# Bonus of a linear-attention chunk moved onto the diagonal of its score tile, with the ninth chunk prepared later and a new written order of the first stage

## The chip, the cores and the metric

The kernel runs on one core of one Trainium2 chip. The metric is the device time of one execution in microseconds. TensorE does the matrix products, VectorE (DVE) and ScalarE (ACT) the elementwise work, GpSimd (POOL) a small part of it, and SyncE (SP) issues most of the transfers. Each engine takes its instructions in the order in which they are written.

## The reference

Two steps follow each other. The first is a linear attention with a decay per channel and a bonus `u` for the current token; the second is a gated feed-forward layer on its output.

```python
for t in range(S):                      # S = 768, batch 4, 8 heads of 48
    cur = np.einsum('bhd,bhe->bhde', u[None] * kt, vt)
    y[:, :, t] = np.einsum('bhd,bhde->bhe', rt, state + cur)
    state = wt[:, :, :, None] * state + np.einsum('bhd,bhe->bhde', kt, vt)
gate = 1.0 / (1.0 + np.exp(-(x @ w_gate)))     # x: 3072 x 384, d_ff = 1536
return gate * (x @ w_val) @ w_out
```

All inputs are float32; the weights come as 64-bit floats and are decoded on the chip.

## The kernel before

Sequence and batch are cut into 24 chunks of 128 tokens; chunk q belongs to batch q % 4 and to row q // 4, so a row is the same 128 tokens of all four batches. Each chunk has two inputs: `pin` (decay, k and r with channels on partitions) and `tok` (r, k and v with tokens on partitions).

The work on one chunk goes in these steps. On DVE, `prep_k` scans the decays and scales k (lines 320 to 331), `fade` ages the state, `prep_r` scans again and scales r (339 to 347). On TensorE, `turn_k` turns k (354), and ACT copies it out (`take_k`). `scores` and `sums` make the score tile and the sums of k times v in the bank pair `pa` (367 to 393). `mask` on DVE multiplies the scores by a strict triangle into the tile `at` (443), `middle` and `keep` bring the state forward. `states` and `mix` (395 to 421) give the chunk's output `py`, `take_y` adds the bonus to it on DVE (463), `turn_x` turns it (467), `take_x` and `rest_x` leave it as a high and a low part in `x`. The bonus is the sum over each head of r, u and k, times v: `bonus1` and `bonus2` are products on POOL (305, 310), `bonus3` a sum on DVE (312), `bonus4` the product with v on POOL (316). `guard` on ACT squares the scans and keeps a sum that is checked at the end.

A row of the feed-forward layer goes over 12 slices f of the hidden dimension: `gate` and `value` (nine matmuls each into `pg` and `pu`), `sigmoid` on ACT, `hidden` on DVE, the split of the product into `hh` (ACT) and `hl` (DVE), and `down` (nine matmuls into `po`). `pg` and `pu` have one bank each.

**The first stage**, up to the end of row 0, is ordered by a planner (class `Plan`, lines 147 to 193). It starts, at each moment of its own reckoning, the ready operation with the lowest rank; ranks come from the list `TURNS` (chunks c and weight slices w), from `LAGS` for the two groups of the feed-forward layer in row 0, and `COMES` is the order of the transfers on SP. `ROOM` says how many buffers a tile has. In this stage each weight slice arrives as 64-bit words (`fetch`), is guarded on ACT (`w_guard`, two passes), decoded on DVE (`w_body`, `w_sign`, `w_tail`) and split (`w_hi` on ACT, `w_lo` on DVE). Chunks 0 to 7 are done here, and the preparation of chunk 8. Group 0 (batches 0 and 1) multiplies by whole float32 weights, line 502; group 1 (batches 2 and 3) by split ones, line 505.

**The loop** over rows 1 to 5 follows a fixed pattern (`blocks`, lines 670 to 706): a slice f has four slots (0 ahead of `gate`, 1 ahead of `value`, 2 ahead of `down` of the slice before, 3 behind it). Each chunk takes three slices; `both` (line 643) does the output of chunk q and the scores of chunk q + 1 among each other in slot 3 of the second slice, `turn_x` is in slot 2 of the third, and `prep_k` of the next chunk opens its first slice. Row 5 has no attention in it.

Of the kernel before, what the change touches and what calls it, by code (L numbers as in the profile page):

```python
# [197 lines left out]
def tile_kernel(ctx: ExitStack, tc: tile.TileContext, dec: bass.AP, tok: bass.AP, wts: bass.AP, u: bass.AP, out: bass.AP):  # L198
# [117 lines left out]
    def bonus4(q):  # L316
        a0 = bank["a0", q].unsqueeze(2).broadcast_to([P, H, D])
        nc.gpsimd.tensor_tensor(out=by_head(bon[q]), in0=by_head(tk[q][:, 2 * DM:]), in1=a0, op=ALU.mult)  # L318
# [124 lines left out]
    def mask(q):  # L443
        att[q] = p1.tile([P, 2, NP, HC], F32, tag="at", name=f"at{q}")
        found = bank["a", q][:, :, :NP * HC].rearrange("a o (p c) -> a o p c", c=HC)
        nc.vector.tensor_tensor(out=att[q], in0=found, in1=after.unsqueeze(1).unsqueeze(1).broadcast_to([P, 2, NP, HC]), op=ALU.mult)
# [16 lines left out]
    def take_y(q):  # L463
        mine = bon[q].rearrange("a (p o e) -> a o p e", o=2, e=D)
        nc.vector.tensor_tensor(out=mine, in0=bank["yy", q], in1=mine, op=ALU.add)  # L465
# [81 lines left out]
    def leave(n):  # L547
        o = stage.tile([P, NKT, B * C], F32, tag="o", name=f"o{n}")
        for j in range(NKT):
# [4 lines left out]
            nc.scalar.dma_start(out[n, j * P:(j + 1) * P], o[:, j])  # L554
# [217 lines left out]
```

## Time and profile before

| | us |
|---|---|
| median of 3 runs (range) | 589.24 (589.06 to 589.64) |
| the profiled execution, its own time | 589.89 |
| its span, first to last instruction | 588.1 |
| TensorE busy in the span | 552.6 (94%) |
| DVE busy | 332.9 (57%) |
| ACT busy | 193.8 (33%) |
| POOL busy | 94.5 (16%) |

The span lies 1.8 us inside the execution's own time. The first stage ends with the last `po` matmul of row 0 at 152.83 us of the span, where the first `pg` of row 1 starts; from there rows 1 to 4 take about 88 us each. Times in rows of the profile count from the span's start. "PEld" is the load of weights into TensorE, which lies beside the matmuls. In a row of the timeline the first number is the start, the second the duration, and the bracket at the end tells how long the engine was idle just before and what ended that.

### The profile page before, as it was taken

Reading aid. Unit: us, or ns where it says so; the run is one execution under the profiler, and the core shown is the slowest. Engines: PE = TensorE matmul, PEld = TensorE weight load, DVE = VectorE, ACT = ScalarE, POOL = GpSimd, SP = SyncE. Lnnn points to the kernel's source line nnn. Section 1 sums busy time; section 2 is a strip of 40 time slices with the busy share of each in tenths; the row PEclk is TensorE's granted clock in tenths of the full one; section 3 lists DMA queues with packets and bytes.
Section 4 is the critical chain, followed back from the end, with each engine's and each line's share of the span. In section 5 each row is a group of like instructions: output and inputs, shape, how many; then the busy total and the mean of one; then the engine's idle time right before and its main releaser. Section 6 shows DMA issues by size and latency. Waiting matters only on the chain.

```text
span 588.1 us, 13530 instructions
## 1 busy us (share of the span) xinstructions
PE 552.6 (94%) x6042; PEld 462.5 (79%) x6042; DVE 332.9 (57%) x485; ACT 193.8 (33%) x359; POOL 94.5 (16%) x86
## 2 busy tenths in 40 slices
PE   2399799999999999999999999999999999999995
PEld 2378588989888888788888788888788888788884
DVE  3989999998555645645645645645645632222121
ACT  2658783324322312322312322312322311311221
POOL 3324232111120210210210211211221200000000
PEclk9999999999999999999999999999999999999999
DMA  8999443305120221330230340230330200100001
GB/s 246 311 326 314 138 173 88 89 6 154 74 90 23 67 88 30 97 107 19 71 88 22 97 114 13 77 90 17 107 109 19 70 1 2 54 3 1 1 1 58
DMA packets 11188, 50.79 MB, mean 86 GB/s; under 512 B 1280, under 2 KB 1408, under 8 KB 9584
## 3 DMA queue, kind: packets, MB, share of 16 engines
q1 hardware_dynamic: 8528, 45.11, 25.0%
q10 hardware_dynamic: 2592, 4.72, 2.2%
q8 instruction: 49, 0.80, 0.6%
q14 instruction: 19, 0.16, 0.1%
HBM read 45.11 MB, written 4.72 MB: 85 GB/s over the span
## 4 chain that ended last, share of the span: by engine, by line
PE 81%; DVE 7%; DMA 4%; issue 3%; ACT 2%; POOL 1%; SPq 0%; ACTq 0%; DVEq 0%; POOLq 0%
PE pg L505 23%; PE pu L505 23%; PE po L545 21%; PE py L405 3%; PE py L418 3%; DMA tok<-tok 3%; PE pa L376 2%; DMA ub<-u 1%; PE pk L357 1%; DVE sg L523 1%; PE pa L389 1%; DVE temp L261 1%; DVE raw L264 1%; DVE w L275 1%; PE po L541 1%
## 5 line engine op out<-in xcount | busy, mean ns | idle before, releaser
L505 PE MATMUL pg<-x,w 128*128 128x512 f32 (+1 forms) x648 | 151.4, 377 | 0.2
L505 PE MATMUL pu<-x,w 128*128 128x512 f32 (+1 forms) x648 | 148.2, 373 | 1.1 <-DVE sg L523 1.1
L523 DVE TENSOR_TENSOR sg<-pu,sg 128x512 f32<-128x512 f32 (+1 forms) x84 | 51.6, 614 | 151.8 <-PE pu L505 143.1
L505 PEld LDWEIGHTS pu<-x,w 128*128 128x128 f32 x648 | 115.2, 188 | 22.6 <-DVE sg L523 1.3
L505 PEld LDWEIGHTS pg<-x,w 128*128 128x128 f32 x648 | 113.4, 188 | 23.4 <-DVE x L490 1.9
L545 PE MATMUL po<-hh,w 128*128 128x512 f32 (+1 forms) x432 | 128.9, 382 | 0.0
L516 ACT ACTIVATE sg<-pg 128x512 f32<-128x512 f32 (+1 forms) x84 | 45.0, 536 | 184.9 <-PE pg L505 175.4
L545 PEld LDWEIGHTS po<-hh,w 128*128 128x128 f32 x432 | 76.7, 189 | 12.7 <-ACT hh L527 0.2
L527 ACT CAST hh<-sg 128x512 fp32r<-128x512 f32 (+1 forms) x72 | 42.1, 584 | 135.1 <-DVE sg L523 135.1
L545 PE MATMUL po<-hl,w 128*128 128x512 f32 (+1 forms) x216 | 80.7, 374 | 0.0
L531 DVE TENSOR_TENSOR hl<-sg,hh 128x512 fp32r<-128x512 f32 (+1 forms) x72 | 49.1, 682 | 42.5 <-ACT hh L527 42.5
L307 POOL TENSOR_TENSOR bon<-tok,ub 128x384 f32<-128x384 f32 x24 | 29.6, 1235 | 228.4 <-DMA tok<-tok 186.5
L545 PEld LDWEIGHTS po<-hl,w 128*128 128x128 f32 x216 | 40.7, 188 | 8.0 <-DVE hl L531 0.4
L318 POOL TENSOR_TENSOR bon<-tok,a 128x384 f32<-128x384 f32 x24 | 23.1, 966 | 144.9 <-DVE a L314 144.9
L310 POOL TENSOR_TENSOR bon<-bon,tok 128x384 f32<-128x384 f32 x24 | 39.3, 1638 | 1.8
L325 DVE TENSOR_TENSOR_SCAN eg<-pin,ends 112x516 f32<-112x516 f32 x24 | 35.7, 1487 | 3.9 <-DMA pin<-dec 3.9
L465 DVE TENSOR_TENSOR bon<-py,bon 128x384 f32<-128x384 f32 x24 | 13.3, 556 | 39.9 <-PE py L418 39.1
L405 PE MATMUL py<-mid,pin 48*64 48x48 f32 x384 | 26.9, 228 | 5.8 <-DVE state L461 5.8
L352 ACT ACTIVATE junk<-eg 112x1032 bf16<-112x1032 f32 x24 | 25.6, 1066 | 19.8 <-DVE eg L342 18.6
L342 DVE TENSOR_TENSOR_SCAN eg<-pin,heads 112x516 f32<-112x516 f32 x24 | 30.2, 1258 | 0.0
L376 PE MATMUL pa<-pin 48*64 48x64 f32 x768 | 26.0, 233 | 4.0 <-DVE pin L347 4.0
L376 PEld LDWEIGHTS pa<-pin 48*64 48x64 f32 x768 | 22.6, 141 | 6.9 <-DVE pin L347 5.4
(67 smaller groups left out, 574.4 us busy)
## 6 DMA issues: line engine op xcount, KB each, us to landing
pin<-dec SPq DMA_DIRECT2D x23, 675.5 KB, 5.2
tok<-tok SPq DMA_DIRECT2D x24, 576.0 KB, 6.3
raw<-wts SPq DMA_DIRECT2D x12, 1152.0 KB, 16.5
y<-o ACTq DMA_DIRECT2D x18, 256.0 KB, 2.0
pin<-dec SPq DMA_DIRECT2D x1, 448.0 KB, 4.1
pin<-dec SPq DMA_DIRECT2D x1, 227.5 KB, 3.0
ub<-u SPq DMA_DIRECT2D x1, 192.0 KB, 7.6
```

The costliest lines, as they stand in the source:

```text
L307: nc.gpsimd.tensor_tensor(out=bon[q], in0=tk[q][:, 0:DM], in1=ub, op=ALU.mult)
L310: nc.gpsimd.tensor_tensor(out=bon[q], in0=bon[q], in1=tk[q][:, DM:2 * DM], op=ALU.mult)
L325: nc.vector.tensor_tensor_scan(out=e[:, 516:0:-1], data0=t[:, 516:0:-1], data1=ends[:, 516:0:-1], initial=0.0, op0=ALU.mult, op1=ALU.add,)
L342: nc.vector.tensor_tensor_scan(out=e[:, WW:WW + 516], data0=t[:, 0:516], data1=heads[:, 0:516], initial=0.0, op0=ALU.mult, op1=ALU.add,)
L376: todo.append(lambda p=p, half=half, o=o, sl=sl: nc.tensor.matmul(t[half, o, p * HC:(p + 1) * HC], lhsT=kk(q)[sl, p, half], rhs=rr(q)[sl, ...
L405: todo[o].append(lambda p=p, s=s, half=half, o=o, sl=sl: nc.tensor.matmul(spots[o][half, p], lhsT=rr(q)[sl, p, half], rhs=(mid if s else r ...
L505: nc.tensor.matmul(t, lhsT=w[f][:, cols], rhs=x[n][:, a, k, spot], start=k == 0 and j == 0, stop=k == NKT - 1 and j == 2)
L516: nc.scalar.activation(sg, hid["g", n, f, i0], AF.Sigmoid)
L523: nc.vector.tensor_tensor(out=sg, in0=hid["u", n, f, i0], in1=sg, op=ALU.mult)
L527: nc.scalar.copy(hh, hid["s", n, f, i0])
L531: nc.vector.tensor_tensor(out=hl, in0=hid["s", n, f, i0], in1=hid["hi", n, f, i0].bitcast(F32), op=ALU.subtract)
L545: nc.tensor.matmul(to, lhsT=w[f][:, cols], rhs=h, start=first and i == 0, stop=last and i == 2, skip_group_check=True)
```

## The change

The bonus becomes part of the score tile. `bonus4` no longer multiplies by v: on POOL it writes the tile `at`, which holds the head's bonus sum on the diagonal of each 64 x 64 block and zero elsewhere (a product of a unit matrix `eye` and the sums, 512 elements in place of 384). `mask` becomes a predicated copy on DVE, which lays the scores over that tile where the strict triangle is one. `take_y` becomes a plain copy on ACT, since `mix` now brings the bonus in. `at` gets two buffers and `mid` one, and `guard` writes over its input.

`u` is no longer spread over the partitions by a transfer of 192 KB: a transfer of one row, a matmul with a row of ones, and a copy on ACT do it. In `both` the second part of the matmuls takes the `sums` alternately by the lower and the upper half of the heads, where it took four of one and then four of the other.

The ninth chunk (q = 8) is prepared within row 1 in place of the first stage. The pattern of the loop is now a table of times in quarter slices: chunks 8 to 11 have their `both` at 11, 21, 32 and 43 (they had 7, 19, 31 and 43), the later ones where they were. `prep_k` of the next chunk is put seven quarters ahead of `both`, `turn_k` five and `prep_r` three. The lists `TURNS` and `COMES`, the lags and some costs of the planner are new. The three output transfers of the last row are issued by SP, not ACT.

```diff
-TURNS = "c0 w0 c1 w1 w2 w3 c2 w4 w5 c3 w6 w7 c4 w8 w9 c5 w10 w11 c6 c7 c8"
-COMES = "p0 t0 ub w0 p1 t1 w1 w2 p2 t2 w3 w4 p3 t3 w5 w6 w7 p4 t4 w8 w9 p5 t5 w10 w11 p6 t6 p7 t7 p8 t8 p9 t9"
+TURNS = "c0 c1 c2 w0 w1 w2 c3 w3 w4 w5 w6 w7 c4 w8 w9 c5 c6 w10 c7 w11"
+COMES = "p0 ub t0 p1 w0 t1 w1 w2 p2 t2 p3 t3 w3 w4 p4 p5 w5 t4 t5 w6 w7 w8 w9 t6 w10 p6 t7 w11 t8 p7 p8 t9 p9"
-LAGS = [0, 4]
+LAGS = [0, -3.0]
+LATE = dict(b3=-8.7, wl=4.0)
+FIRST = [11, 21, 32, 43]
...
     def bonus4(q):
-        a0 = bank["a0", q].unsqueeze(2).broadcast_to([P, H, D])
-        nc.gpsimd.tensor_tensor(out=by_head(bon[q]), in0=by_head(tk[q][:, 2 * DM:]), in1=a0, op=ALU.mult)
+        shape = [P, 2, NP, HC]
+        att[q] = p2.tile(shape, F32, tag="at", name=f"at{q}")
+        a0 = bank["a0", q].rearrange("a (p o) -> a o p", o=2).unsqueeze(3).broadcast_to(shape)
+        nc.gpsimd.tensor_tensor(out=att[q], in0=eye.unsqueeze(1).unsqueeze(1).broadcast_to(shape), in1=a0, op=ALU.mult)
...
     def mask(q):
-        att[q] = p1.tile([P, 2, NP, HC], F32, tag="at", name=f"at{q}")
         found = bank["a", q][:, :, :NP * HC].rearrange("a o (p c) -> a o p c", c=HC)
-        nc.vector.tensor_tensor(out=att[q], in0=found, in1=after.unsqueeze(1).unsqueeze(1).broadcast_to([P, 2, NP, HC]), op=ALU.mult)
+        nc.vector.copy_predicated(att[q], after.bitcast(I32).unsqueeze(1).unsqueeze(1).broadcast_to([P, 2, NP, HC]), found)
...
     def take_y(q):
-        mine = bon[q].rearrange("a (p o e) -> a o p e", o=2, e=D)
-        nc.vector.tensor_tensor(out=mine, in0=bank["yy", q], in1=mine, op=ALU.add)
+        nc.scalar.copy(bon[q].rearrange("a (p o e) -> a o p e", o=2, e=D), bank["yy", q])
...
-            nc.scalar.dma_start(out[n, j * P:(j + 1) * P], o[:, j])
+            (nc.sync if n == NC_ - 1 else nc.scalar).dma_start(out[n, j * P:(j + 1) * P], o[:, j])
...
+    def spread():
+        bank["u"] = att_bank("spread")
+        nc.tensor.matmul(bank["u"][:, :DM], lhsT=line[:, :P], rhs=line[:, P:], start=True, stop=True)
...
-        early, late = (more[0::4] + more[1::4], more[2::4] + more[3::4]) if q + 1 < NG - B else (more, [])
+        early, late = ([f for i, f in enumerate(more) if i // 2 % 2 == s] for s in range(2)) if q + 1 < NG - B else (more, [])
...
+    def prepare(q, early, turn, late):
+        at(early, bonus1, q)
+        at(early, bonus2, q)
+        at(early, prep_k, q)
+        at(early, fade, q)
+        at(turn, turn_k, q)
+        at(turn, take_k, q)
+        at(late, prep_r, q)
+        at(late, guard, q)
+        at(late, bonus3, q)
+        at(late, bonus4, q)
...
+    visit = {q: (q - start) // B * row + (7 + 12 * (q % B) if q >= start + B else FIRST[q - start]) for q in range(start, NG)}
+    prepare(start, 0, 2, 3)
+    at(6, section1, start)
+    settle(start, 6)
+    for q, time in visit.items():
+        if q + 1 < NG:
+            if q == start:
+                prepare(q + 1, 5, 7, 8)
+            else:
+                prepare(q + 1, time - 7, time - 5, time - 3)
+        at(time, both, q)
+        at(time, take_y, q)
...
+        at(time + 3, turn_x, q)
+        at(time + 3, take_x, q)
+        at(time + 3, rest_x, q)
```

Three places show how instructions moved. The first is the head of SP's queue: `raw` is a weight slice, `pin` and `tok` the inputs of a chunk. Before:

```order
L286 DMA pin_100<-dec 112x520
L287 DMA pin_100<-dec 112x1024
L294 DMA tok_103<-tok 128x1152
L575 DMA ub<-u 128x384
L246 DMA raw_110<-wts 128x1152
L289 DMA pin_159<-dec 112x1544
L294 DMA tok_215<-tok 128x1152
L246 DMA raw_219<-wts 128x1152
L246 DMA raw_243<-wts 128x1152
```

Of the change:

```order
L291 DMA pin_105<-dec 112x520
L292 DMA pin_105<-dec 112x1024
L583 DMA line<-u 1x384
L299 DMA tok_109<-tok 128x1152
L294 DMA pin_117<-dec 112x1544
L251 DMA raw_129<-wts 128x1152
L299 DMA tok_178<-tok 128x1152
L251 DMA raw_235<-wts 128x1152
L251 DMA raw_283<-wts 128x1152
```

The second chunk's `pin` now stands ahead of the first weight slice, and the row of `u` takes the place of the spread one.

The second place is ACT's queue up to the first sigmoid's table load. `kT`, `mid` and `whole` belong to chunks, `sq` to the guard of a weight slice (two rows each). Before, from behind the first chunk's `mid` on:

```order
L253 ACTIVATE sq_169,acc_s<-raw_110 128x1152
L254 ACTIVATE sq_169,acc_t<-sq_169 128x1152
L485 ACTIVATE whole,acc_x<-px_222 128x3x128
L272 CAST w_232<-raw_110 128x1152
L361 COPY kT_245<-pk_238 128x448
L253 ACTIVATE sq_249,acc_s<-raw_219 128x1152
L254 ACTIVATE sq_249,acc_t<-sq_249 128x1152
L455 COPY mid_293<-pa_254 112x192
L352 ACTIVATE junk_295,acc_d<-eg_228 112x1032
L253 ACTIVATE sq_299,acc_s<-raw_243 128x1152
L254 ACTIVATE sq_299,acc_t<-sq_299 128x1152
L485 ACTIVATE whole,acc_x<-px_353 128x3x128
```

Of the change, the same stretch:

```order
L469 COPY bon_127<-py_191 128x2x4x48
L358 ACTIVATE eg_172,acc_d<-eg_172 112x2x516
L489 ACTIVATE whole,acc_x<-px_244 128x3x128
L460 COPY mid_287<-pa_249 112x192
L277 CAST w_291<-raw_129 128x1152
L258 ACTIVATE sq_298,acc_s<-raw_235 128x1152
L259 ACTIVATE sq_298,acc_t<-sq_298 128x1152
L258 ACTIVATE sq_347,acc_s<-raw_283 128x1152
L259 ACTIVATE sq_347,acc_t<-sq_347 128x1152
L469 COPY bon_239<-py_306 128x2x4x48
L489 ACTIVATE whole,acc_x<-px_362 128x3x128
L520 ACT_TABLE_LOAD
```

The copies of `py` into `bon` are new on ACT; the one of chunk 1 stands behind the guards of the second and third weight slices, and the one of chunk 0 behind the guard of the first.

The third place is in row 1, between the `both` of chunk 8 and the fifth slice. On TensorE, of the change (`px` is `turn_x` of chunk 8, `pk` is `turn_k` of chunk 10):

```order
L509 MATMUL pg_0_3_2074<-x_1086,w_673 128x512 x9
L509 MATMUL pu_0_3_2086<-x_1086,w_673 128x512 x9
L474 MATMUL px_2101<-ident,bon_1797 128x128 x3
L549 MATMUL po_0_1920<-hh_0_2_1969,w_600 128x512 x2
L549 MATMUL po_0_1920<-hl_0_2_1971,w_600 128x512
L549 MATMUL po_1_1921<-hh_0_2_1969,w_600 128x512 x2
L549 MATMUL po_1_1921<-hl_0_2_1971,w_600 128x512
L549 MATMUL po_2_1922<-hh_0_2_1969,w_600 128x512 x2
L549 MATMUL po_2_1922<-hl_0_2_1971,w_600 128x512
L363 MATMUL pk_2126<-ident,pin_2070 128x112 x4
L509 MATMUL pg_0_4_2133<-x_1086,w_722 128x512 x9
L509 MATMUL pu_0_4_2145<-x_1086,w_722 128x512 x9
```

On DVE, of the change, the same stretch (`eg` and `heads` are the scan of chunk 10):

```order
L527 TENSOR_TENSOR sg_0_3_2084<-pu_0_3_2086,sg_0_3_2084 128x512
L535 TENSOR_TENSOR hl_0_3_2099<-sg_0_3_2084,hh_0_3_2097 128x512
L494 TENSOR_TENSOR x_2105<-px_2101,x_2105 128x3x128
L332 SCALAR_TENSOR_TENSOR eg_2111<-pin_2070,ends 112x516
L336 RECIPROCAL heads<-eg_2111 112x4
L338 TENSOR_TENSOR pin_2070<-pin_2070,eg_2111 112x512
L344 TENSOR_TENSOR ready_2115<-state_103,eg_2111 112x192
L527 TENSOR_TENSOR sg_0_4_2143<-pu_0_4_2145,sg_0_4_2143 128x512
```

DVE's order is that of before at this point, but on TensorE the `pg` and `pu` of the next slice, which stood between this `down` and `turn_k` (first `pk` row) before, now stand behind it.

More of the change, by code (lines that the diff above doesn't have):

```diff
@@ L223, in tile_kernel @@
     nc.gpsimd.memset(after, 1.0)
-    for s in range(2):
-        part = after[s * HC:(s + 1) * HC]
+    eye = const.tile([P, HC], F32, name="eye")
+    for s, half in enumerate(HALVES):
         nc.gpsimd.affine_select(
-            out=part, in_=part, pattern=[[1, HC]], compare_op=ALU.is_gt, fill=0.0, base=0, channel_multiplier=-1,
+            out=after[half], in_=after[half], pattern=[[1, HC]], compare_op=ALU.is_gt, fill=0.0, base=0, channel_multiplier=-1,
         )
+        nc.gpsimd.tensor_copy(eye[half], ident[half, half])
     ub = const.tile([P, DM], F32, name="ub")
@@ L451, in middle @@
     def middle(q):
-        mid[q] = p2.tile([L, NP, D], F32, tag="mid", name=f"mid{q}")
+        mid[q] = p1.tile([L, NP, D], F32, tag="mid", name=f"mid{q}")
         if q < B:
@@ L573, in add @@
         plan.add(name, engine, cost, after, rank, f and (lambda: f(*args)), take, give)
-    add("ub", "SP", 0.6, [], comes["ub"], lambda: nc.sync.dma_start(ub, u.partition_broadcast(P)))
+    def spread():
+        bank["u"] = att_bank("spread")
+        nc.tensor.matmul(bank["u"][:, :DM], lhsT=line[:, :P], rhs=line[:, P:], start=True, stop=True)
+    add("line", "SP", 0.1, [], comes["ub"], lambda: nc.sync.dma_start(line[:, P:], u.unsqueeze(0)))
+    add("wide", "PE", 0.65, ["line"], -1, spread, take=["bank"])
+    add("ub", "ACT", 0.5, ["wide"], -1, lambda: nc.scalar.copy(ub, bank["u"][:, :DM]), give=["bank"])
     ahead = (R0 + 1) * B
@@ L580, in tile_kernel @@
         add(f"tok{q}", "SP", 2.1, [], comes[f"t{q}"], load_tok, q, take=["tok"])
-        if q > ahead:
+        if q >= ahead:
             continue
-        add(f"b1_{q}", "POOL", 1.4, [f"tok{q}", "ub"], k, bonus1, q, take=["bon"])
+        add(f"b1_{q}", "POOL", 1.2, [f"tok{q}", "ub"], k, bonus1, q, take=["bon"])
         add(f"b2_{q}", "POOL", 1.15, [f"b1_{q}"], k, bonus2, q)
-        add(f"b3_{q}", "DVE", 0.55, [f"b2_{q}"], k + 0.3, bonus3, q)
-        add(f"b4_{q}", "POOL", 1.45, [f"b3_{q}"], k, bonus4, q)
+        add(f"b3_{q}", "DVE", 0.55, [f"b2_{q}"], k + LATE["b3"], bonus3, q)
+        add(f"b4_{q}", "POOL", 1.4, [f"b3_{q}"], k, bonus4, q, take=["at"])
         add(f"pk{q}", "DVE", 2.1, [f"pin{q}"], k, prep_k, q, take=["eg"])
@@ new lines, in at, with settle @@
+    def at(time, f, *a):
+        todo.setdefault(time, []).append((f, a))
+    def prepare(q, early, turn, late):
[9 more added lines that the diff above has]
+        at(late, bonus4, q)
+    def settle(q, time):
+        at(time, mask, q)
+        at(time, middle, q)
+        if q < NG - B:
+            at(time, keep, q)
@@ L735, in tile_kernel @@
+    assert not todo, todo
     down(*last.pop())
```

109 lines of the change are left out of this document (39 added, 70 removed).

## The prediction

> **What bounds the kernel now.** I read the busy time by stretches, then the timeline of the first 40 us, then one chunk of the loop, then the tail. First view: stretch and length, busy us (instructions) of PE, PEld, DVE, ACT, POOL, granted clock, DMA share, GB/s.
>
> ```profile
> 0.00:14.50 14.50, 3.88 (x84) 3.40 (x84) 5.30 (x8) 3.19 (x5) 5.34 (x17) 1.00 0.88 247
> 14.50:34.00 19.50, 9.10 (x222) 7.31 (x220) 18.55 (x19) 12.23 (x22) 7.62 (x5) 1.00 1.01 327
> 34.00:60.00 26.00, 25.42 (x239) 21.22 (x239) 23.54 (x31) 19.23 (x33) 8.25 (x5) 1.00 0.97 313
> 60.00:90.00 30.00, 25.76 (x421) 22.32 (x422) 28.48 (x37) 22.00 (x39) 7.21 (x6) 1.00 0.37 136
> 90.00:120.00 30.00, 28.75 (x332) 26.49 (x331) 28.62 (x38) 10.55 (x21) 5.92 (x5) 1.00 0.31 87
> 120.00:147.00 27.00, 26.81 (x479) 25.13 (x480) 25.11 (x43) 10.61 (x24) 3.90 (x4) 1.00 0.31 87
> 235.00:322.00 87.00, 86.95 (x988) 71.65 (x987) 45.91 (x70) 24.48 (x47) 15.15 (x12) 1.00 0.22 66
> ```
>
> The loop (last line) is TensorE without a gap; only fewer or faster matmuls, or a new wait, move it. The first stage has two bounds. Up to 34 us TensorE mostly waits. From 14.5 to 120 us DVE is busy 99.2 of 105.5 us; TensorE, which has work all along, still idles 0.58 + 4.24 + 1.25 + 0.19 = 6.3 us between 34 and 147 us. So a relief of DVE is worth at most 6.3 us there; more comes only from an earlier first feed-forward matmul. The timeline up to that:
>
> ```profile
> 9.89 0.99 POOL L307 TENSOR_TENSOR bon<-tok,ub 128x384 f32<-128x384 f32 x1 [6.45 <-DMA ub<-u]
> 11.98 0.55 DVE L314 TENSOR_REDUCE a<-bon 128x8 f32<-128x384 f32 x1 [4.02 <-POOL bon L310]
> 14.53 1.30 ACT L253 ACTIVATE sq<-raw 128x1152 f32<-128x1152 f32 x1 [4.17 <-DMA raw<-wts]
> 17.02 0.19 ACT L254 ACTIVATION_READ_ACCUMULATOR sq<-sq 128x1 f32 x1
> 18.34 1.23 DVE L325 TENSOR_TENSOR_SCAN eg<-pin,ends 112x516 f32<-112x516 f32 x1
> 22.75 1.25 ACT L253 ACTIVATE sq<-raw 128x1152 f32<-128x1152 f32 x1 [0.20 <-DMA raw<-wts]
> 28.19 1.24 ACT L253 ACTIVATE sq<-raw 128x1152 f32<-128x1152 f32 x1
> 31.54 0.56 DVE L465 TENSOR_TENSOR bon<-py,bon 128x384 f32<-128x384 f32 x1 [0.75 <-PE py L418]
> 33.09 0.49 ACT L485 ACTIVATE whole<-px 128x384 f32<-128x384 f32 x1 [2.28 <-PE px L470]
> 33.73 2.93 PE L502 MATMUL pg<-whole,raw 128*128 128x256 f32 x6 [0.67 <-ACT whole L485]
> 39.70 1.48 PE L502 MATMUL pg<-whole,raw 128*128 128x256 f32 x6
> ```
>
> The feed-forward work starts at 33.73 because chunk 1 is late: its scan starts at 18.34, its output is taken at 31.54.
>
> **The start.** The row of `u` should land near 5 us, behind the first `pin`. Its matmul is two records of 384 columns at the slow pace of the row at 33.73 (2.93 / 6 per 256 columns): 1.5 us, and a copy like that at 33.09 takes 0.5. The spread `u` is there near 7.2, not 9.75, and the bonus sum of 11.98 comes near 9.8. Chunk 1's scan follows at 10.2, eight us sooner. That gain does not reach the output. The second `pin` (0.69 MB) is now ahead of the first weight slice and the spread row (0.2 MB) gone: at 327 GB/s the slice lands about 1 us later, at 15.5. ACT guards it for 2.7 us (14.53 to 17.21) ahead of the copy of `py`, so chunk 0's output comes at 18.8, its transposes (0.9 at the slow pace) end at 19.8, and chunk 1's scores, written behind them on TensorE, only then begin; they and the sums take 2.2. Then ACT: `mid`, the split of slice 0 (1.25) to 23.7, guard of slice 1 to 26.4, guard of slice 2 to 29.2 if that has landed (before it had by 28.19), and only then chunk 1's copy: 0.5, transposes 0.9, copy 0.5, start at 31.3. I take **2.4 us gained**; bounds 4.2 (ACT never waits for a slice) and 0.
>
> **DVE in the first stage.**
>
> ```profile
> L465 DVE TENSOR_TENSOR bon<-py,bon 128x384 f32<-128x384 f32 x24 | 13.3, 556 | 39.9 <-PE py L418 39.1 <-POOL bon L318 0.7
> L446 DVE TENSOR_TENSOR at<-pa,after 128x512 f32<-128x512 f32 x24 | 16.4, 681 | 0.2 <-ACT mid L455 0.2
> L318 POOL TENSOR_TENSOR bon<-tok,a 128x384 f32<-128x384 f32 x24 | 23.1, 966 | 144.9 <-DVE a L314 144.9
> 140.35 1.77 DVE L325 TENSOR_TENSOR_SCAN eg<-pin,ends 112x516 f32<-112x516 f32 x1
> 142.25 0.67 DVE L331 TENSOR_TENSOR pin<-pin,eg 112x512 f32<-112x512 f32 x1
> 144.34 1.22 DVE L342 TENSOR_TENSOR_SCAN eg<-pin,heads 112x516 f32<-112x516 f32 x1
> 145.60 0.69 DVE L347 TENSOR_TENSOR pin<-pin,eg 112x512 f32<-112x512 f32 x1
> 147.26 0.54 DVE L314 TENSOR_REDUCE a<-bon 128x8 f32<-128x384 f32 x1
> ```
>
> Eight takes of `y` leave DVE: 8 x 0.556 = 4.4 us; chunk 8's preparation too (the last five rows): 4.9 us. But the latter lay behind 140 us, where TensorE was full, so it closes no gap. The predicated copy has no row. Below it lies the masked product of the same shape (0.68), above it the scan, the slowest row of this width (1.22); I take 0.68, the same shape and sources, so nothing; at 1.22 it is 8 x 0.54 = 4.3 us more on the engine that bounds. `bonus4` is 512 elements for 384: 0.97 x 4/3 = 1.3 us on a POOL that is 16% busy; uncovered, the mask would wait for it. `y` on ACT costs 0.5 and is hidden where ACT idles. The guard keeps its 1032 elements. So of the 6.3 us idle, 4.4 could go by sums; the planner's list also puts both transfers of chunks 4 and 5 around the sixth slice, which costs some of it. I take **1.8 us gained**, bounds 6.3 gained and 3 lost. Chunk 8's transposes leave this stage and come back in row 1: nothing.
>
> **Row 1 of the loop.** Chunk 10's `turn_k` now follows the `down` directly, while DVE still has the same queue ahead of it. The same place before:
>
> ```profile
> 215.75 0.49 PE L470 MATMUL px<-ident,bon 128*128 128x128 f32 x3
> 218.17 2.21 PE L505 MATMUL pg<-x,w 128*128 128x512 f32 x9
> 217.40 1.38 DVE L531 TENSOR_TENSOR hl<-sg,hh 128x512 fp32r<-128x512 f32 x1 [0.69 <-ACT hh L527]
> 218.70 0.55 DVE L490 TENSOR_TENSOR x<-px,x 128x384 fp32r<-128x384 f32 x1
> 219.16 1.57 DVE L325 TENSOR_TENSOR_SCAN eg<-pin,ends 112x516 f32<-112x516 f32 x1
> 220.87 0.66 DVE L331 TENSOR_TENSOR pin<-pin,eg 112x512 f32<-112x512 f32 x1
> ```
>
> TensorE is done with `down` at 218.17, and k is scaled at 221.53. Before, the next `pg` and `pu` (4.1 us) lay between; now TensorE waits 3.4 us, and everything is queued behind. Without POOL's work beside it (`hl` 0.69, scan 1.22) it is 2.3. I take **3.3 us lost**. The other three chunks of row 1 have `pg` and `pu`, or `pu` and `down`, in between.
>
> **The order of the sums** in `both`: first and last start of the first 32 matmuls, for chunk 10, and for chunk 22, where half the sums are left out and the rest already alternate.
>
> ```profile
> 208.94 0.25 PE L405 MATMUL py<-ready,pin 48*64 48x48 f32 x1
> 210.03 0.22 PE L376 MATMUL pa<-pin 48*64 48x64 f32 x1
> 473.62 0.25 PE L405 MATMUL py<-ready,pin 48*64 48x48 f32 x1
> 474.55 0.23 PE L376 MATMUL pa<-pin 48*64 48x64 f32 x2
> ```
>
> 1.09 against 0.93 us: 0.16 for the order, in 11 chunks (8 to 18) **1.8 us gained**; the part behind it may give as much again (3.5) or the order nothing. The Trainium skill (TensorE: Matmul & The Clock Gate, The mechanism) says that weight loads pass running matmuls only where the row group differs; alternating the output half leaves the row groups as they are, so by it the sum would lack the 1.8 and the time be 587.4. The trace's 0.16 speaks against it.
>
> **The tail.**
>
> ```profile
> 580.39 1.75 ACTq L554 DMA_DIRECT2D y<-o  x2
> 580.46 0.69 DVE L551 COPY o<-po 128x512 f32<-128x512 f32 x1 [1.28 <-PE po L545]
> 582.18 0.59 ACT L553 COPY o<-po 128x512 f32<-128x512 f32 x1 [1.82 <-issue]
> ```
>
> ACT's second transfer waits for DVE's copy (to 581.15), and the third copy sits behind it until 582.18. With SP issuing, it starts near 581.2: **0.95 us gained**; SP's issue may cost up to 0.2 more.
>
> **Sum** against the profiled execution (589.89; span 588.1 and 1.8 around it): 589.89 - 2.4 - 1.8 + 3.3 - 0.95 - 1.8 = 586.2. The median of the runs lies 0.65 below the profiled one: **585.6**.
>
> **Rivals.**
> (a) DVE's relief closes all 6.3 us rather than 1.8: 581.1. For it: DVE is 94% busy and TensorE is full wherever DVE is not. Against: ACT, 22 of 30 us busy from 60 to 90, gets the copies.
> (b) The predicated copy goes at the scan's pace, 4.3 us more on DVE: 589.9, no gain in all.
> (c) Slower: ACT's queue at the start. Chunk 1's copy stands behind the guard of the third slice, so each us that this slice lands past 26.4 is a us on the start and on the end. At 33, when the queue ahead of it moves at 200 GB/s, the start is at 38 and the time 592.2; it is slower than before from a landing at 30 on. For it: the transfers are saturated (share 1.01). Against: the slice had landed by 28.19 before, with 0.2 MB more ahead of it.
> (d) The wait in row 1 slows TensorE's clock. Between the rows at 33.73 and 39.70 lie two groups and four transposes of about 3.5 us at the later pace, so a slow restart costs 2.5: 588.1. Against: gaps of 1 to 2 us in the first stage had no slow rows behind them, but none there is as long. The Trainium skill (same page, What's actually happening) has the clock halved after an idle window of about 3.4 us, which the forecast wait just misses; it gives this rival its chance.
>
> **How the numbers follow.** Forecast 0.42 (its own range 582.5 to 588), (a) 0.20, (b) 0.13, (c) 0.15, (d) 0.10. Differences under 0.2%, 1.2 us, can't be told from none. Faster: the forecast, (a) and half of (d), 0.67; same: (b) and the rest of (d), 0.18; slower: (c), 0.15. The range runs from (a) to just beyond (b), 580.8 to 590.2, and leaves out most of (c).
>
> **What would show it.** First `pg` of row 0 near 31.3, behind ACT's copy of `whole`; the first `pg` of row 1 near 148.6, not 152.83; a gap of about 3 us ahead of the third `pk` group of row 1; the predicated copy at 0.68; `both` shorter by 0.16 up to chunk 18; the last copy 1 us sooner. I am wrong if the start moves by more than 2 us from this, or the loop's gap is absent.

## The result

The changed kernel takes **595.22 us** (median of 8 runs, 592.72 to 595.91), the kernel before 589.15 (8 runs, 588.11 to 591.55): a ratio of 1.0087, 95% interval 1.0065 to 1.0109. It is slower by 5.1 us by that ratio, 6.1 by the medians, where a gain of 3.6 was forecast. The profiled execution took 595.33, its span is 593.2 (before 588.1).

Where the 5.1 us of span come from is read from two kinds of landmark, the first gate group of row 1 and, in each later row, the first copy of the row before it out of `po`. Lengths are from one such copy to the next, in us; the line of the changed kernel's profile that gives the first landmark stands below.

| | row 1 starts | row 1 | row 2 | row 3 | row 4 | row 5 |
|---|---|---|---|---|---|---|
| before | 152.95 | 93.44 | 88.43 | 88.24 | 86.48 | 70.03 |
| changed | 146.16 | 100.65 | 88.98 | 88.98 | 87.99 | 71.99 |
| difference | -6.79 | +7.21 | +0.55 | +0.74 | +1.51 | +1.96 |

These sum to 5.18; the spans differ by 5.13, since 0.05 is given back behind the last of these copies. The first stage gained more than forecast, row 1 lost more, and every row behind it is longer too, row 5 included, in which nothing but feed-forward matmuls is left and in which the change edits nothing.

The changed kernel's timeline, start, length, engine, line, operation and tiles: the first weight load of the first feed-forward group (forecast 31.3), and the first gate group of row 1 (forecast 148.6, before 152.95).

```profile
31.55 2.21 PEld L506 LDWEIGHTS pg<-whole,raw 128*128 128x128 f32 x6 [1.07 <-ACT whole L489]
...
146.16 2.49 PE L509 MATMUL pg<-x,w 128*128 128x512 f32 x9
```

The same timeline where chunk 10's k is turned in row 1:

```profile
174.70 0.40 PE L549 MATMUL po<-hl,w 128*128 128x512 f32 x1
...
175.23 1.56 DVE L332 TENSOR_TENSOR_SCAN eg<-pin,ends 112x516 f32<-112x516 f32 x1
...
176.92 1.21 DVE L338 TENSOR_TENSOR pin<-pin,eg 112x512 f32<-112x512 f32 x1
178.23 0.98 PE L363 MATMUL pk<-ident,pin 112*128 112x112 f32 x4 [3.13 <-issue]
178.89 3.44 PE L509 MATMUL pg<-x,w 128*128 128x512 f32 x9
182.17 1.09 PE L509 MATMUL pu<-x,w 128*128 128x512 f32 x4
```

TensorE waits 3.13 us for DVE, as forecast (3.3). But the gate group behind it takes 3.28 us to the next start instead of some 2.2, and the transposes 0.66 instead of 0.35: 1.4 us more. Two stretches (start and end, length, busy us of PE, PEld, DVE, ACT, POOL, granted clock, DMA share, GB/s) show the granted clock below 1 there:

```profile
175.00:180.00 5.00, 1.86 (x8) 1.61 (x8) 3.36 (x5) 0.53 (x1) 2.50 (x2) 0.79 0.02 5
180.00:185.00 5.00, 5.00 (x21) 3.98 (x20) 0.47 (x1) 0.60 (x1) 0.00 (x0) 0.87 0.00 0
```

What was not forecast is plainest in row 5. There the timeline of the kernel before has

```profile
542.16 2.20 PE L505 MATMUL pg<-x,w 128*128 128x512 f32 x9
544.20 2.20 PE L505 MATMUL pu<-x,w 128*128 128x512 f32 x9
548.28 2.20 PE L505 MATMUL pg<-x,w 128*128 128x512 f32 x9
```

and that of the changed one

```profile
539.95 2.26 PE L509 MATMUL pg<-x,w 128*128 128x512 f32 x9
542.05 2.26 PE L509 MATMUL pu<-x,w 128*128 128x512 f32 x9
546.25 2.26 PE L509 MATMUL pg<-x,w 128*128 128x512 f32 x9
```

From start to start nine matmuls take 2.04 us before and 2.10 now (226.7 and 233.3 ns each), a slice 6.12 and 6.30, at a granted clock of 1.00 in both and with no gap. The groups by line, tile and shape (count, busy us, mean ns of one) say the same; before:

```profile
L505 PE MATMUL pu<-x,w 128*128 128x512 f32 x540 | 132.4, 390 | 0.0
```

and changed, with the added operations of the other engines:

```profile
L509 PE MATMUL pu<-x,w 128*128 128x512 f32 x540 | 135.8, 396 | 0.0
L451 DVE COPY_PREDICATED at<-after,pa 128x512 f32<-128x512 int32 x24 | 17.6, 732 | 20.8 <-PE py L411 16.2 <-PE pa L382 4.6
L325 POOL TENSOR_TENSOR at<-eye,a 128x512 f32<-128x512 f32 x24 | 29.0, 1211 | 135.8 <-DVE a L319 135.8
L469 ACT COPY bon<-py 128x384 f32<-128x384 f32 x24 | 11.5, 479 | 53.6 <-PE py L424 53.5
```

The tail of the changed kernel:

```profile
585.56 2.49 SPq L558 DMA_DIRECT2D y<-o  x3
586.35 0.59 ACT L557 COPY o<-po 128x512 f32<-128x512 f32 x1 [0.81 <-PE po L549]
```

The last copy starts 0.43 us behind the last matmul's start (585.92), where it was 1.45 (580.73 to 582.18). Yet from that matmul's start to the end of the span it is 7.3 us in both.

### The profile page after: what moved, and what is told of

Its sections match the earlier page's. It is cut to its first block, busy times and chain, and to the rows that moved or that the text cites. A ratio compares the mean times of both kernels' runs of the same rounds, so it can differ in the third digit from the quotient of the medians.

```text
span 593.2 us, 13560 instructions
## 1 busy us (share of the span) xinstructions
PE 559.7 (94%) x6044; PEld 460.8 (78%) x6044; DVE 327.0 (55%) x461; ACT 204.6 (34%) x384; POOL 101.6 (17%) x89
## 4 chain that ended last, share of the span: by engine, by line
PE 89%; DVE 5%; issue 2%; DMA 2%; ACT 1%; SPq 0%; DVEq 0%
PE pg L509 24%; PE pu L509 23%; PE po L549 22%; PE py L424 3%; PE py L411 3%; PE pg L506 3%; PE pu L506 2%; PE po L545 2%; PE pa L382 2%; DMA pin<-dec 2%; PE pk L363 2%; PE pa L395 2%; PE px L474 1%; DVE w L280 1%; DVE hl L535 1%
## 5 line engine op out<-in xcount | busy, mean ns | idle before, releaser
L509 PE MATMUL pg<-x,w 128*128 128x512 f32 (+1 forms) x648 | 156.4, 385 | 1.1 <-DVE x L494 0.7
L509 PE MATMUL pu<-x,w 128*128 128x512 f32 (+1 forms) x648 | 151.3, 378 | 0.3 <-DVE sg L527 0.3
L535 DVE TENSOR_TENSOR hl<-sg,hh 128x512 fp32r<-128x512 f32 (+1 forms) x72 | 52.0, 722 | 41.8 <-ACT hh L531 41.6
L325 POOL TENSOR_TENSOR at<-eye,a 128x512 f32<-128x512 f32 x24 | 29.0, 1211 | 135.8 <-DVE a L319 135.8
L358 ACT ACTIVATE eg<-eg 112x1032 f32<-112x1032 f32 x24 | 25.6, 1068 | 33.3 <-DVE pin L354 32.0
L469 ACT COPY bon<-py 128x384 f32<-128x384 f32 x24 | 11.5, 479 | 53.6 <-PE py L424 53.5
L451 DVE COPY_PREDICATED at<-after,pa 128x512 f32<-128x512 int32 x24 | 17.6, 732 | 20.8 <-PE py L411 16.2
L411 PEld LDWEIGHTS py<-mid,pin 48*64 48x64 f32 x384 | 22.4, 140 | 5.4 <-ACT sq L259 4.5
```

The costliest lines, as they stand in the source:

```text
L411: todo[o].append(lambda p=p, s=s, half=half, o=o, sl=sl: nc.tensor.matmul(spots[o][half, p], lhsT=rr(q)[sl, p, half], rhs=(mid if s else r ...
L509: nc.tensor.matmul(t, lhsT=w[f][:, cols], rhs=x[n][:, a, k, spot], start=k == 0 and j == 0, stop=k == NKT - 1 and j == 2)
L535: nc.vector.tensor_tensor(out=hl, in0=hid["s", n, f, i0], in1=hid["hi", n, f, i0].bitcast(F32), op=ALU.subtract)
```

## The experiments

The search began with the matmuls. Their weights, sizes, PSUM banks and order in a slice are the same in both kernels. What differs is where tiles lie: the change drops `junk` (2,064 bytes per partition), adds `eye` (256), gives `at` (2,048) a second buffer and leaves `mid` (768) one of two. Counting each tile in whole multiples of 32 bytes, so `junk` as 2,080, what lies behind all of them moves by 256 - 2,080 + 2,048 - 768 = -544 bytes, which is 8.5 times 64. The tiles of the moving operands (`x`, `hh`, `hl`, and `sg` behind them) lie there. The weight tiles lie behind `eye` alone and move by 256, 4 times 64. So weights and moving operands, which both began at multiples of 64 bytes by the addresses that I read in the built program of before, now stand 32 bytes apart, counted modulo 64. No run records an address; what the runs can show is what a shift does. All experiments on addresses add one or two unused tiles of 8 floats, 32 bytes per partition, and nothing else.

**e1: the changed kernel, moved back by 32 bytes.**

```
     p2 = own.enter_context(tc.tile_pool(name="p2", bufs=2))
+    p1.tile([P, 8], F32, name="pad")
```

> The changed kernel with one unused tile of 8 floats (32 bytes per partition) put first into the pool p1, so that everything behind it, x, hh, hl and sg among it, lies 32 bytes further and begins on a multiple of 64 bytes again, as in the kernel before. Nothing else differs. Theory A (address): nine matmuls of 512 columns take 2.10 us in the changed kernel and 2.04 before because their moving operand begins 32 bytes off a multiple of 64. It expects 2.04 again in rows 2 to 5, 27 x 6.7 ns = 0.18 us less per slice, 10.8 us less over 60 slices: about 584.5. Rival B (state): the wait in row 1 at 175 to 178 us, with the granted clock at 0.79, left TensorE a little slower for the rest of the execution. It expects 2.10 still and about 595.

Measured: 587.5 us (10 runs), ratio to before 0.9959 (0.9939 to 0.9978). Row 5:

```profile
545.35 2.20 PE L510 MATMUL pg<-x,w 128*128 128x512 f32 x9
547.38 2.20 PE L510 MATMUL pu<-x,w 128*128 128x512 f32 x9
```

The groups are back at 2.03 to 2.04 and a slice at 6.12, with the wait and the slow stretch of row 1 still there; theory B falls. Rows 1 to 5 are 1.60, 1.41, 1.42, 1.52 and 1.93 us shorter than in the changed kernel, **7.9 us** in all. The 10.8 expected counts every slice at the 0.18 of row 5. There it holds (1.93 for 11 slices); rows 1 to 4 lose a quarter less. The two traces show which groups: in row 2, six of the nine groups of a chunk take 0.05 to 0.06 us less in e1. The other three stand directly behind small matmuls (the gate group behind `both`, the `down` behind `turn_x` and the one behind `turn_k`). They take 2.16 to 2.19 us in e1 already and 2.18 to 2.20 in the changed kernel, so at most 0.02 less. Why they do is not shown.

**e2: the kernel before, with the same tile.** There it pushes the moving operands off.

```
     p2 = own.enter_context(tc.tile_pool(name="p2", bufs=2))
+    p1.tile([P, 8], F32, name="pad")
```

> The kernel before with the same unused tile of 32 bytes put first into p1, which there moves x, hh, hl, sg, pin and tok off the multiple of 64 bytes. No instruction differs. Theory A (address): nine matmuls of 512 columns go from 2.04 to 2.10 us, the time to about 589.2 + 10.8 = 600, although this kernel has no wait in row 1. Rival B (state): 2.04 and 589.2 as before. Rival C (the weights' place or the instruction stream is what slows the changed kernel): 589.2 too.

Measured: 598.17 us, ratio 1.0141 (1.0111 to 1.0170). Row 5:

```profile
540.70 2.26 PE L506 MATMUL pg<-x,w 128*128 128x512 f32 x9
542.80 2.26 PE L506 MATMUL pu<-x,w 128*128 128x512 f32 x9
```

2.10 again, with no instruction of the kernel before changed and no wait over 0.6 us in row 1. Row 5 is 71.99 us long, to the hundredth that of the changed kernel. Theory B falls, and theory C as the one cause: here neither the weights nor the instructions moved. (That the weights' place counts as well comes out in e8.)

**e3: cover for chunk 10's transposes** (on e1).

```
-FIRST = [11, 21, 32, 43]
+FIRST = [11, 23, 32, 43]
```

> The padded changed kernel with chunk 9's turn in row 1 two slots later (the second number of FIRST 23, not 21), so that a gate and a value group, and not a down group, lie between the scaling of k and the transposes of chunk 10. The wait of 3.1 us ahead of the third group of pk in row 1 should go, and with it the stretch at half clock behind it (2.5 us by the groups of 2.87 us). Expected against the padded kernel: 5 us less if the clock's part is real and all of it goes, 3 us less if only the wait counts, 0 if the wait turns up at another place in row 1: about 579.5, 581.5 or 584.5.

Measured: 586.94 us, ratio 0.9948 (0.9927 to 0.9969); row 1 is 98.81 us, 99.05 in e1. The third outcome: the wait went to chunk 11.

```profile
200.57 0.63 PE L364 MATMUL pk<-ident,pin 112*128 112x112 f32 x4 [3.15 <-DVE x L495]
200.94 3.89 PE L510 MATMUL pg<-x,w 128*128 128x512 f32 x9
204.67 1.55 PE L510 MATMUL pu<-x,w 128*128 128x512 f32 x6
```

Chunk 9's output is now turned one `down` group ahead of chunk 11's `turn_k`. Both use the one bank `turn`, and it is released only by DVE's `x` row (L495), which stands behind chunk 11's scan. Again the gate group behind the wait is slow, 3.73 us.

**e4: only the operands of `down` moved** (the kernel before).

```
     stage = own.enter_context(tc.tile_pool(name="late", bufs=1))
+    stage.tile([P, 8], F32, name="pad")
```

> The kernel before with the unused 32 bytes put first into the pool that is opened behind the first stage: only hh, hl, sg and the output tile move off the multiple of 64 bytes; x, the weights and all else stay. Theory A (the moving operand's own address): the nine down matmuls of a slice (moving hh and hl) go from 0.68 to 0.70 us per three, gate and value groups (moving x) stay at 2.04; 9 x 6.7 ns x 60 = 3.6 us more, 592.8. If any shift slows all of them, 600; if the address of hh and hl doesn't matter, 589.2.

Measured: 593.19 us, ratio 1.0045 (1.0021 to 1.0069). The gate and value groups of a slice in row 5, and the next gate group:

```profile
544.95 2.24 PE L505 MATMUL pg<-x,w 128*128 128x512 f32 x9
547.03 2.20 PE L505 MATMUL pu<-x,w 128*128 128x512 f32 x9
551.17 2.24 PE L505 MATMUL pg<-x,w 128*128 128x512 f32 x9
```

From `pu` to the next `pg`, nine value and nine `down` matmuls, it is 4.14 us, where it is 4.08 before and 4.20 in the changed kernel: half of the loss, and so the nine `down` matmuls alone. `pg` takes 2.08, 0.04 more than before, though neither `x` nor the weights moved; nothing tried here explains it. A slice is 6.22, between 6.12 and 6.30. So moving `hh` and `hl` alone slows the matmuls that stream them, and the gate group behind them by less.

**e5: chunks of row 1 spread otherwise** (on e1).

```
-FIRST = [11, 21, 32, 43]
+FIRST = [10, 20, 31, 43]
```

> The padded changed kernel with FIRST = [10, 20, 31, 43]: the transposes of chunk 8's output then stand a whole value and down group ahead of chunk 10's turn_k, chunk 10's and 11's k are scaled a value and a down group ahead of theirs, and chunk 10's pin is issued one slot sooner too. Theory: the wait of 3.4 us in row 1 came from too little TensorE work between what DVE has to do (the rest of x, then the scaling of k) and turn_k; in e3 it only moved to chunk 11, whose turn_k stood one down group behind chunk 9's transposes. Expected: no PE gap over 1 us in row 1, no slow groups behind it, row 1 5 us shorter than in e1 and e3 (93.5 to 94.5 from first copy of one row's output to that of the next, where they have 99), the time near 582. Rival: row 1 of the changed kernel holds too much for any order (chunk 8's preparation too), the wait turns up at a third place, and the time stays at 586 to 588.

Measured: **584.09 us**, ratio **0.9894** (0.9867 to 0.9920), faster than both kernels. A stretch of 5 us where e1 waited:

```profile
175.00:180.00 5.00, 4.25 (x21) 3.28 (x20) 4.28 (x7) 1.65 (x3) 0.73 (x1) 1.00 0.00 0
```

The long wait and the slow clock are gone; 0.75 us of wait are left here, 0.36 ahead of chunk 9's transposes, and at the merged section of chunk 8 TensorE is busy for 2.78 of 4 us: one wait of 1.22, where none over 1 us was expected. Row 1 is 96.24 us, 2.8 shorter than in e1 and not the 5 expected. Half of what the long wait gave up came back as short ones: the direction was right, the size wrong.

**e6: the order of the sums as before** (on e5).

```
-early, late = ([f for i, f in enumerate(more) if i // 2 % 2 == s] for s in range(2)) if ...
+early, late = (more[0::4] + more[1::4], more[2::4] + more[3::4]) if ...
```

> As e5, with the sums in the merged section of a chunk in the order that they had before. The prediction's term: 0.16 us a chunk, 11 chunks, 1.8 us in all. By the row lengths of e1 against those of before (87.57 against 88.43 and 87.56 against 88.24 in rows 2 and 3, equal in row 4 where the order is the same) it is about 0.2 a chunk: rows 2 and 3 are 0.7 to 0.9 us longer than in e5, row 4 the same, the time 1.8 to 2.4 us more. If the rows differ for another reason (the copy of y on ACT, the mask's copy), no row changes.

Measured: 587.24 us, ratio 0.9939 (0.9919 to 0.9959). Rows 1 to 4 are 97.10, 88.42, 88.24 and 86.46 us against 96.24, 87.58, 87.57 and 86.48 in e5. Rows 1 to 3 lose 0.86, 0.84 and 0.67, together 2.4, 0.2 for a chunk; row 4, where the order is the same, loses nothing. The medians lie 3.2 apart and the spans of the two profiles 3.7; what exceeds the 2.4 lies there ahead of row 1 (0.4) and behind the last matmul (0.9), outside the rows where the order of the sums is at work. Rows 2 to 4 are those of the kernel before to the hundredth or two (88.43, 88.24, 86.48): nothing else that the change does in these rows costs or saves time that can be seen.

**e7: ACT issues the last transfers** (on e5).

```
-(nc.sync if n == NC_ - 1 else nc.scalar).dma_start(out[n, j * P:(j + 1) * P], o[:, j])
+nc.scalar.dma_start(out[n, j * P:(j + 1) * P], o[:, j])
```

> As e5, with ACT and not SP issuing the last three output transfers. The prediction's term: 0.95 us lost, since the third copy sits behind a transfer's issue. By the traces from the last matmul's start to the end of the span it is 7.37 us in the kernel before and 7.28, 7.12 and 7.32 in those with SP: the copy comes 1 us sooner, but SP issues later behind it. Expected: the last copy 1 us later, the span's end 0.1 to 0.5 us later.

Measured: 584.19 us, ratio 0.9893 (0.9860 to 0.9926), 0.1 from e5.

```profile
574.49 1.81 ACTq L559 DMA_DIRECT2D y<-o  x2
576.34 0.59 ACT L558 COPY o<-po 128x512 f32<-128x512 f32 x1 [1.88 <-issue]
576.95 0.34 ACTq L559 DMA_DIRECT2D y<-o  x1
```

In e5 the same place reads

```profile
574.32 2.23 SPq L559 DMA_DIRECT2D y<-o  x3
...
575.09 0.59 ACT L558 COPY o<-po 128x512 f32<-128x512 f32 x1 [0.80 <-PE po L550]
```

The copy begins 1.5 us behind the last matmul's start here and 0.43 in e5, but to the end of the span it is 7.3 and 7.2 us. Counted from that matmul (574.84 here, 574.66 in e5) the queue is done with its issues at 2.45 and 1.89 us, so that of the 1.07 us by which the copy is sooner 0.56 are left behind the issues and 0.1 at the end of the span. That 0.1 is below the scatter: over the fourteen profiles the stretch from the last matmul to the end is 7.1 to 8.2 us where SP issues and 7.3 to 8.2 where ACT does.

**e8: only the weights moved** (the kernel before; the second tile puts the rest back on its multiple of 64).

```
     state = [const.tile([L, NP, D], F32, name=f"state{b}") for b in range(B)]
+    const.tile([P, 8], F32, name="skew")
...
     p2 = own.enter_context(tc.tile_pool(name="p2", bufs=2))
+    p1.tile([P, 8], F32, name="pad")
```

> The kernel before with two unused tiles of 32 bytes, one behind the states and one first in p1: the weight tiles and eg, kT begin 32 bytes off or on a multiple of 64 the other way, while x, hh, hl, sg, pin and tok stay on a multiple of 64. If only the moving operand's address matters: matmuls of 512 columns at 2.04 and 0.68, the time 589. If the stationary operand's address matters as well: 2.10 and 0.70, 597.

Measured: 597.1 us, ratio 1.0108 (1.0074 to 1.0141). Row 5:

```profile
541.62 2.26 PE L507 MATMUL pg<-x,w 128*128 128x512 f32 x9
543.72 2.26 PE L507 MATMUL pu<-x,w 128*128 128x512 f32 x9
```

The moving operand lies as before, and it is 2.10 all the same. So theory A as I had put it, the moving operand's own address, falls too.

**e9: weights and moving operands both moved** (the kernel before).

```
     state = [const.tile([L, NP, D], F32, name=f"state{b}") for b in range(B)]
+    const.tile([P, 8], F32, name="skew")
```

> The kernel before with one unused tile of 32 bytes behind the states, so that the weights AND x, hh, hl, sg, pin, tok all begin 32 bytes off a multiple of 64; nothing else differs. In e2 (moving operands off, weights on) and in e8 (weights off, moving operands on) nine matmuls of 512 columns took 2.10 us, with both on 2.04. Theory A1 (each operand has to begin on a multiple of 64): 2.10 or more, and 597 or more. Theory A2 (what counts is how the two stand to each other, weights being loaded while the operand streams): 2.04, and 589 to 590.

Measured: 590.18 us, ratio **0.9995** (0.9978 to 1.0013). Row 5:

```profile
542.72 2.20 PE L506 MATMUL pg<-x,w 128*128 128x512 f32 x9
544.76 2.20 PE L506 MATMUL pu<-x,w 128*128 128x512 f32 x9
```

2.04 and a slice at 6.12, with both 32 bytes off. Not an operand's own address counts, but how the weights and the moving operand stand to each other: alike modulo 64, 226.7 ns; 32 apart, 233.3. The gate group of e4 is the one that does not fit: 2.08 with `x` and weights where they were. Whether the loading of the next weights, which runs under each matmul, is what collides is argued from this and not shown.

**e10: the eight copies of y in the first stage on DVE** (on e5; the planner is told, so that it also orders the stage anew).

```
-        nc.scalar.copy(bon[q].rearrange(...), bank["yy", q])
+        (nc.vector.tensor_copy if q < ahead else nc.scalar.copy)(bon[q].rearrange(...), bank["yy", q])
...
-add(f"y{q}", "ACT", 0.5, ...
+add(f"y{q}", "DVE", 0.56, ...
```

> As e5, with the eight copies of the first stage's y on DVE and not ACT (the planner told so, 0.56 us each; in the loop they stay on ACT). The prediction's term for DVE's relief was 1.8 us, of which the eight takes of y were the working part (4.4 us of DVE time), with bounds of 6.3 gained and 3 lost. Measured, row 1 starts near 146 in the changed kernels and at 150.5 to 153 in those with the order of before. If the relief is what closed TensorE's gaps, row 1 starts 2 to 4.4 us later than in e5 (145.58) and the time rises by as much; if the new lists and the earlier start did it, less than 1 us.

Measured: 593.79 us, ratio 1.0059 (1.0038 to 1.0080). Row 1 starts at 153.28, 7.7 us later than in e5, more than the 4.4 us that were moved. The stretch from 31 to 146 us of e10:

```profile
31.00:146.00 115.00, 104.96 (x1465) 93.88 (x1465) 104.58 (x143) 61.84 (x113) 29.09 (x18) 0.99 0.45 161
```

and of e5:

```profile
31.00:146.00 115.00, 111.20 (x1512) 100.14 (x1511) 103.07 (x139) 66.07 (x123) 28.32 (x18) 1.00 0.46 159
```

TensorE idles 10.0 us instead of 3.8. About 1.7 of the 7.7 are clock: behind a wait of 2.24 us the granted clock is 0.50 from 53.05 to 56.46 us in e10, and e5 has no such stretch. The lists were chosen with the copies on ACT, so this prices the copies with lists that no longer fit them, not the copies alone.

**e11: the lists of the kernel before** (on e5): `TURNS`, `COMES`, `LAGS` as in the diff's lines with a minus.

```
-LATE = dict(b3=-8.7, wl=4.0)
+LATE = dict(b3=0.3, wl=4.0)
```

> As e5, with the lists TURNS, COMES and LAGS and the rank of the bonus sums as they were in the kernel before; everything else (predicated copy, bonus diagonal, y on ACT, u spread by TensorE, chunk 8 in the loop) as changed. The prediction gave the lists nothing of their own but a cost where two chunks' transfers stand around a slice. If the gain of the first stage lies in the work moved off DVE, row 1 starts within 1.5 us of e5's 145.58; if the lists carry it, 3 to 7 us later, near 149 to 153.

Measured: 590.71 us, ratio 0.9998 (0.9979 to 1.0017). Row 1 starts at 151.81.

```profile
31.00:146.00 115.00, 107.73 (x1477) 96.08 (x1476) 99.60 (x134) 65.81 (x122) 27.74 (x19) 1.00 0.45 152
```

With everything else changed and the old lists, little is left of the gain in the first stage: 1.1 us against before. TensorE idles 7.3 us. So neither the lists nor the lighter DVE carries the gain by itself: with either undone row 1 starts between 151.8 and 153.3, with both near 146. That rests on one profile each, and the times of e5 and e11 (6.6 us apart) agree with it. One profile of this stage is worth no more than some 3 us: seven executions with one and the same first stage (the changed kernel, e1, e3, e5, e6, e7, e12) start row 1 between 145.58 and 148.75, median 146.02, five with that of the kernel before (before, e2, e4, e8, e9) between 150.52 and 153.13, median 152.73. The two do not overlap.

**e12: chunk 9 prepared a slot sooner** (on e5).

```
-prepare(q + 1, 5, 7, 8)
+prepare(q + 1, 4, 6, 7)
```

> As e5, with chunk 9 prepared one slot sooner in row 1 (slots 4, 6 and 7, not 5, 7 and 8). In e5 row 1 still waits 1.2 us at the merged section of chunk 8 (TensorE busy 2.78 of 4 us from 162 to 166, where k and r of chunk 9 must be ready), 0.36 ahead of chunk 9's transposes and 0.75 ahead of chunk 10's. Expected: the first two go, 1.0 to 1.5 us less, about 582.8 where e5 has 584.1 (row 1 94.8 to 95.3 instead of 96.24). Rival: DVE is the limit there and the wait moves ahead of the first section's work: no change.

Measured: 585.76 us, ratio 0.9916 (0.9887 to 0.9945); row 1 is 96.28 us, as in e5. The rival was right in that the wait moves and nothing is gained:

```profile
158.55 1.45 DVE L333 TENSOR_TENSOR_SCAN eg<-pin,ends 112x516 f32<-112x516 f32 x1 [0.76 <-ACT eg L359]
160.13 1.21 DVE L339 TENSOR_TENSOR pin<-pin,eg 112x512 f32<-112x512 f32 x1
161.44 0.57 PE L364 MATMUL pk<-ident,pin 112*128 112x112 f32 x4 [2.60 <-issue]
```

The two short waits became one of 2.60 ahead of chunk 9's transposes. It is not DVE's busy time alone that fills it: DVE is busy 10.4 of 13 us from 153 to 166. Chunk 9's scan waits 0.76 us for `eg`, which has one buffer and which ACT's guard of chunk 8 still holds, and the scaling of k takes 1.21 us beside POOL's products, where that of chunk 8, at 150.32, takes 0.66. The same two rows stand in e5 (0.76 and 1.23). A second buffer for `eg` was not tried.

## Why the prediction was wrong

**What it left out decided.** The sum has no term for the lines of `ROOM`, `eye` and `junk`: they compute nothing, so I gave them nothing. The step that failed is "only fewer or faster matmuls, or a new wait, move it", said of the loop: the same matmuls may also go slower, and that case had no term, no rival and no chance. The lines move the moving operands 32 bytes against the weights, matmuls of 512 columns go from 226.7 to 233.3 ns, and that costs 7.9 us (e1 against the changed kernel, row by row; e2 against before 8.4, of which 0.5 is a wait). With 7.9 added to 585.6 the forecast would have been 593.5. That this lies near the 595.2 measured is in part luck: the first stage gained 2.6 more than forecast and row 1 lost more than forecast, and these two nearly cancel. Nothing in the profile of before could show the cost of the addresses. The two built programs could have shown that they move, but not at what price; e2 is the first run that shows the price by itself.

Step by step, the rest:

- *Start of row 0, 2.4 gained (31.3).* 31.55, so 2.2 gained: right, within 0.25, and rival (c) did not occur. The chain behind it was only in part the one forecast. Chunk 1's scan started at 12.40 and not 10.2, since its `pin` landed only then, and the bonus sum came at 11.48, not 9.8. When ACT's queue was through with the guards, the copy of chunk 1's output still waited for TensorE, which had waited for the mask on DVE:

```profile
29.44 0.48 ACT L469 COPY bon<-py 128x384 f32<-128x384 f32 x1 [0.20 <-PE py L424]
```

  Two chains ended within 0.2 us of each other, and only the one by ACT's queue was in the forecast; that it sufficed was luck.
- *DVE's relief in the first stage, 1.8 gained.* Right in size. From the first feed-forward matmul to row 1 TensorE idles 6.3 us before and 4.4 in the changed kernel, so 1.9 are closed; by the means of the seven and five executions it is 1.9 too (5.7 and 3.8). So rival (a), all idle closed, is not what happened. But with the start 4.2 were forecast for row 1's start, and 6.8 is what the two profiles show (6.7 by the medians of seven and five). The rest is TensorE's busy time in this stage, 112.9 us before and 110.3 now, for which the sum had no term. Of these 2.7 us about 1.5 are clock: a group of six takes 2.9 us at first and 1.5 later, and that slow pace lasts for 3.0 us of feed-forward work now and lasted for 5.9 before. Chunk 8's transposes are 0.3, and 0.9 stays open. The step "the planner's list ... costs some of it" failed as well: by e11 the lists are a condition of the gain, not a cost, and by e10, with the lists as they are, so is the copy on ACT.
- *Predicated copy at 0.68, bonus diagonal at 1.3.* 0.73 and 1.21: right, nearest to the row of the same shape. Rival (b) falls.
- *Row 1's wait, 3.3 lost.* 3.13 in the changed kernel and 3.40 in e1: right in place and size. But rival (d) came with it. The clock did slow, which cost 1.4 us (1.7 in e1 and e3) and not the 2.5 worked out there; I had given it a tenth because a wait of 3.3 was just short of the idle window that the Trainium skill names (TensorE: Matmul & The Clock Gate, What's actually happening). The other argument against it, that shorter gaps in the first stage had no slow rows behind them, held for the one execution that I had read: in e2, e4, e8 and e9, whose first stage has the same instructions, the clock slows behind them. I took cover for one chunk to be the whole story. e3, e5 and e12 show that the wait moves to another chunk or splits, by the shared bank in e3, by DVE's queue and the one `eg` buffer in e5 and e12: of the orders tried the best gets back 2.8 of the 5 us.
- *Order of the sums, 1.8 gained.* 2.4 (e6): right in kind, 0.2 a chunk where 0.16 was read. The rule of the Trainium skill that was weighed there (the same page, The mechanism), by which nothing would come of it, is not borne out.
- *Tail, 0.95 gained.* The copy came 1.0 sooner, as said; the end at most 0.1 (e7 against e5: 7.3 and 7.2 us), which is within the scatter. The step that failed is to take the start of the last copy for the end. What the span waits for is the last transfer: by the trace's landings it lands 4.49 us behind the last matmul's start in e5 and 4.55 in e7. "SP's issue may cost up to 0.2 more" was far too little.

Put together with the measured sizes: first stage -6.8, row 1's wait 3.1 and its slow clock 1.4, the sums -2.4, tail -0.1 and addresses 7.9 give +3.1 of the 5.1. Of the rest 0.7 is a longer wait for DVE's `x` at the first gate group of row 2, by the weight loads of the changed kernel

```profile
241.01 1.69 PEld L509 LDWEIGHTS pg<-x,w 128*128 128x128 f32 x8 [1.18 <-DVE x L494]
```

and of the kernel before

```profile
240.64 1.69 PEld L505 LDWEIGHTS pg<-x,w 128*128 128x128 f32 x8 [0.48 <-DVE x L490]
```

This wait comes and goes between executions: TensorE itself stops there for 0.75 us in the changed kernel and not before, for 0.53 in e2 and 0.82 in e9, and not in e1 or e5. Another 0.35 are the transposes that chunk 8's preparation brings into row 1 (what left the first stage is already in its 6.8), and 0.23 the wait ahead of chunk 9's. About 0.7 stays unexplained.

## What to carry to other kernels

When buffers are added, dropped or given another count, compare the addresses of what TensorE reads, before and after: weights and moving operands that stood alike modulo 64 bytes should still stand alike, and here an unused tile of 32 bytes put it right. A TensorE group of one shape that took longer in a stretch without edits was the sign of it, and such a group should be the first thing compared between two traces. A wait that is moved by giving one chunk more cover may only change its place; look at what holds the shared bank, the shared buffer and the queue next. An end is measured to the landing of the last transfer.
